# A linear-attention layer and its feed-forward part on one core: a third output buffer, a last batch done row tile by row tile, and a last output sent in halves

## The chip, the cores and the metric

The kernel runs on one core of a Trainium2 chip. The metric is the device time of one execution, in microseconds (us). TensorE (PE) does the matrix products and writes them into PSUM; VectorE (DVE) and ScalarE (ACT) copy, gate and split what PE produced; SyncE (SP) and ACT issue the transfers (DMAs); GpSimd (POOL) only clears memory here.

## The reference

Two steps are computed. The first is a recurrence over 768 positions for 4 batches, 8 heads and a head size of 48, with a state of 48x48 per head. The second is a feed-forward part on the 3072 resulting rows of 384:

```python
for t in range(S):
    cur = einsum('bhd,bhe->bhde', u[None] * k[t], v[t])
    y[t] = einsum('bhd,bhde->bhe', r[t], state + cur)
    state = w * state + einsum('bhd,bhe->bhde', k[t], v[t])
x = y as (4 * 768, 384)
h = x @ w_in                     # 384 -> 2048
g = h * tanh(softplus(h))
out = g @ w_out                  # 2048 -> 384
```

All inputs and the output are float32; the two weights arrive as float64.

## The kernel before

**Tiling.** The 768 positions are cut into 6 groups of 128, and the 4 batches make 4 steps in each group, so a group has 512 columns (`T`). The recurrence is done in chunks of 128 positions by products. For each group, the feed-forward part runs over 16 tiles of 128 hidden rows (`NF`), numbered `n = 16 * g + f` over the whole kernel, 0 to 95. `up_tile(n)` makes one hidden tile `hp` in PSUM; `evacuate` copies it to `hb` (line 890); two tiles make a batch (`FB = 2`, batches 0 to 47), and `gate` applies three activations to a batch (`fa`, lines 785, 788, 791), multiplies (`gate1`, line 798), and, from the second group on, splits the result into a high part `gh` (`gate2`, line 802) and a low part `gl` (`gate3`, line 806). `down_tile(n)` adds the tile's products to three accumulators `acc0`, `acc1`, `acc2` in PSUM, one for each 128 rows of the output (row tile `mt`). In the split form each product is three matmuls (`three`, line 752): high weight by high part, high weight by low part, low weight by high part. `down_tile` comes six tiles (`LAG`) after `up_tile`.

**Outputs.** After the last tile of a group, `output(g, mt)` copies each accumulator to an SBUF tile `ob` (line 825, on ACT or DVE) and sends it with a DMA of 256 KB issued by ACT (line 826). `ob` comes from a pool with two buffers, so the third `ob` of a group takes the buffer of the first, and its copy has to wait until the first one's transfer has landed. Before the first product of the next group, PE needs the accumulators copied out.

**Order.** The order on every engine is written out at build time: `Flow` is a small planner in which each piece of work is a generator that yields the names of events it waits for and a cost in us for one or more engines (`pe(...)`, `act(...)`, `dve(...)`). The planner picks an engine by the time it is free plus the cost, with DVE's cost weighted by 1.5, and emits the instructions in that order; the costs serve this planning alone. At run time each engine goes through its list in order and waits on semaphores.

**Other users.** The tile `we` (two buffers of 128x768) is used in the first group when weights are converted (line 358), and from tile 44 to tile 89 by `check_range`, which reads a weight block every third tile (ACT line 304, DVE line 306). SP issues all loads. ACT and SP, like the other engines, end with a load of a flag (line 986), a branch on it (line 988; the other side is a fallback for unusual inputs, not taken here) and waits for all transfers and engines (lines 988 and 1152).

The recurrence's results are read from PSUM tiles `yt` and `yh` by `finish` (ACT line 700, DVE line 702), and the state update reads another part of `yt` (DVE line 643).

Of the kernel before, what the change touches and what calls it, by code (L numbers as in the profile page):

```python
# [10 lines left out]
F32 = mybir.dt.float32  # L11
# [13 lines left out]
NC = S // C  # L25
NS = NC * B
DM, DFF = H * D, 2048
KT = DM // 128
NF = DFF // 128
# [3 lines left out]
WG = 2  # L33
WE = 384 * WG
NW = NF // WG
# [15 lines left out]
T = B * C  # L51
FB = 2
# [30 lines left out]
LAG = 6  # L83
# [8 lines left out]
L_ATT, L_V, L_IN, L_OUT, L_GATE, L_EVAC, L_PUT, L_FIN = 3, -2, 6, 8, 2, 12, 9, 4  # L92
# [63 lines left out]
def dve(cols, fast=False):  # L156
    return {"dve": 0.14 + cols / (1900 if fast else 950)}


def act(cols):  # L160
    return {"act": 0.1 + cols / 1060}


def pe(us):
    return {"pe": us}
# [3 lines left out]
def rwkv_mish_kernel(ctx, tc, rkT, rkN, vN, wT, w_in, w_out, consts, rkF, vF, wF, uF, outT):  # L169
    nc = tc.nc  # L170
    const = ctx.enter_context(tc.tile_pool(name="const", bufs=1))
    stage = ctx.enter_context(tc.tile_pool(name="stage", bufs=2))
# [107 lines left out]
    flow = Flow(FREE)  # L280
    flow.events["wt"] = 3.5
    at = LAND0
# [48 lines left out]
    raws, whole, parts = {}, {}, {}  # L331
# [407 lines left out]
    def hp_free(cost=None):  # L739

        if cost is None:
            if len(hp_log) >= 2:
                yield hp_log[-2]
            return
        while len(hp_log) >= 2 and hp_log[-2] not in flow.events:
            yield hp_log[-2]
            yield pe(cost)


    def three(out, wh, wl, mh, ml, first, last):  # L750
        for n, (a, m) in enumerate(((wh, mh), (wh, ml), (wl, mh))):
            nc.tensor.matmul(out, lhsT=a, rhs=m, start=first and n == 0, stop=last and n == 2)  # L752
# [4 lines left out]
    def new_batch(T, x, f, n):  # L757

        o = Batch()
        o.T, o.x, o.f, o.n = T, x, f, n  # L760
        o.hb = by_tile(o, work.tile([128, COLS], F32, name="hb", tag="hb", bufs=3))
        return o

    def by_tile(o, t):
        return t[:, : o.n * o.T].rearrange("p (j t) -> p j t", j=o.n)

    def up(o, j, event=None):
        f, T = o.f + j, o.T
        hp = hp_tile("hp", event)
        for k in range(KT):  # L770
            fs = slice((k * WG + f % WG) * 128, (k * WG + f % WG + 1) * 128)
            if o.x.dtype == F32:
                e = whole[0, f // WG]
                nc.tensor.matmul(hp[:, :T], lhsT=e[:, fs], rhs=o.x[:, k, :, 0], start=k == 0, stop=k == KT - 1)  # L774
            else:
                w = parts[0, f // WG]
                three(
                    hp[:, :T], w[:, 0, fs], w[:, 1, fs], o.x[:, k, :, 0], o.x[:, k, :, 1], k == 0, k == KT - 1
                )
        return hp[:, :T]  # L780


    def act1(o):
        o.g = by_tile(o, work.tile([128, COLS], F32, name="fa", tag="fa", bufs=1))
        nc.scalar.activation(o.g, o.hb, AF.Sigmoid, bias=bias_ln2, scale=1.0)  # L785

    def act2(o):
        nc.scalar.activation(o.g, o.g, AF.Arctan)  # L788

    def act3(o):  # L790
        nc.scalar.activation(o.g, o.g, AF.Sin, scale=2.0)  # L791

    def gate1(o):
        if o.x.dtype == F32:
            o.gf = by_tile(o, work.tile([128, COLS], F32, name="gf", tag="gh"))
            nc.vector.tensor_tensor(out=o.gf, in0=o.hb, in1=o.g, op=ALU.mult)  # L796
        else:
            nc.vector.tensor_tensor(out=o.hb, in0=o.hb, in1=o.g, op=ALU.mult)  # L798

    def gate2(o, engine):  # L800
        o.gh = by_tile(o, work.tile([128, COLS], F32R, name="gh", tag="gh"))
        (nc.scalar.copy if engine == "act" else nc.vector.tensor_copy)(out=o.gh, in_=o.hb)  # L802

    def gate3(o):
        o.gl = by_tile(o, work.tile([128, COLS], F32R, name="gl", tag="gl"))
        nc.vector.tensor_tensor(out=o.gl, in0=o.hb, in1=o.gh.bitcast(F32), op=ALU.subtract)  # L806

    accs = {}

    def down(o, j):  # L810
        f = o.f + j
        for mt in range(KT):
# [6 lines left out]
            else:  # L819
                w = parts[1, f // WG]  # L820
                three(a, w[:, 0, ws], w[:, 1, ws], o.gh[:, j], o.gl[:, j], f == 0, f == NF - 1)

    def put(engine, mt, T, cols):
        ob = stage.tile([128, 512], F32, name="ob", tag="ob")
        (nc.scalar.copy if engine == "act" else nc.vector.tensor_copy)(out=ob[:, :T], in_=accs[mt][:, :T])  # L825
        nc.scalar.dma_start(outT[mt * 128 : (mt + 1) * 128, cols], ob[:, :T])


    batches = {}

    def tile_cost(g):
        return pe(9 * (T + 30) / 2400 if g else 3 * 4 * T / 2400)
# [22 lines left out]
    def emitted(n, h):  # L855
        g, f = divmod(n, NF)
        b, j = divmod(n, FB)
        if b not in batches:
            batches[b] = new_batch(T, xs[g], f - j, FB)
        o = batches[b]  # L860
        flow.start(evacuate(n, o, j, h), n - L_EVAC)
        if j == FB - 1:
            flow.start(gate(b, o, range(n - j, n + 1)), n - L_GATE)
        if f == NF - 1:
            flow.set(f"ups{g}")
        if not g and f % WG == WG - 1:
            flow.set(f"used0,{f // WG}")

    def up_tile(n):
        g, f = divmod(n, NF)  # L870
        b, j = divmod(n, FB)
        if n < len(EARLY):
            yield f"early{n}"
            return
        if f == 0:
            for s in range(B):
                yield f"x{g * B + s}"
        if j == 0 and b >= 3:
            yield f"gated{b - 3}"
        yield f"w0,{f // WG}" if g else f"e0,{f // WG}"  # L880
        yield from hp_free()
        yield tile_cost(g)
        yield from hp_free(0.0)
        if j == 0:
            batches[b] = new_batch(T, xs[g], f, FB)
        emitted(n, up(batches[b], j, f"h{n}"))
# [6 lines left out]
    def gate(b, o, tiles):  # L893
        for n in tiles:
            yield f"h{n}"
        if not b:
            yield "TKn"
        if b >= 1:
            yield f"mixed{b - 1}"
        t = act(o.n * o.T)["act"]  # L900
        yield {"act": t + 1.28}
        act1(o)
        yield {"act": t}
        act2(o)
        yield {"act": t + 1.28}
        act3(o)
        if b >= 2:
            yield f"downs{b - 2}"
        cols = o.n * o.T
        yield dve(cols)  # L910
        gate1(o)
        flow.set(f"mixed{b}")
        if b >= NF // FB:
            engine = yield {**act(cols), **dve(cols, True)}
            gate2(o, engine)
            yield dve(cols)
            gate3(o)
        for k in range(o.n):
            flow.set(f"g{FB * b + k}")
        flow.set(f"gated{b}")  # L920

    def down_tile(n):
        g, f = divmod(n, NF)
        b, j = divmod(n, FB)
        if f == 0:
            if g:
                for mt in range(KT):
                    yield f"put{g - 1},{mt}"
            else:
                for k in range(2, len(EARLY)):  # L930
                    yield f"h{k}"
        yield f"w1,{f // WG}" if g else f"e1,{f // WG}"
        yield f"g{n}"
        yield tile_cost(g)
        down(batches[b], j)
        if j == FB - 1:
            flow.set(f"downs{b}")
        if not g and f % WG == WG - 1:
            flow.set(f"used1,{f // WG}")
        if f == NF - 1:  # L940
            for mt in range(KT):
                flow.start(output(g, mt), n - L_PUT)

    def output(g, mt):
        engine = yield {**dve(T), **act(T)}
        put(engine, mt, T, slice(g * T, g * T + T))
        flow.set(f"put{g},{mt}")


    def ffn():  # L950
        last = NC * NF
        for n in range(last + LAG):
            if n < last:
                yield from up_tile(n)
                flow.set(f"u{n}")
            if n >= LAG:
                yield from down_tile(n - LAG)

    load_early()
    for s in range(NS):  # L960
# [13 lines left out]
    for c in range(len(W_ORDER)):  # L974
        i, f = W_ORDER[c]
        flow.start(convert(c), (-999.5, -998.5)[c] if c < 2 else f * WG + (LAG - L_OUT if i else -L_IN) + c / 1000, 0.0)
        flow.start(split(c), NF + f * WG + (LAG - L_OUT if i else -L_IN) + c / 1000, 0.0)
    flow.start(ffn(), 1000, 0.0)
    flow.run()
    assert not flow.parked, list(flow.parked)  # L980
# [7 lines left out]
    with tc.If(in_range < 128 * N_FLAGS):  # L988
# [48 lines left out]
        with tc.tile_pool(name="any2", bufs=1) as work:  # L1037
# [4 lines left out]
            for c, key in enumerate(W_ORDER):  # L1042
                w = parts[key]
# [6 lines left out]
                    out=eu, in0=top, scalar=0x80000000, in1=eu, op0=ALU.bitwise_and, op1=ALU.bitwise_xor  # L1050
# [8 lines left out]
            for b in range(B):  # L1059
                with tc.For_i(0, S, 128) as t0:  # L1060
# [5 lines left out]
                    for k in range(KT):  # L1066
                        nc.tensor.transpose(
                            out=t[:, k * 128 : (k + 1) * 128], in_=xt[:, k].rearrange("t q e -> t (q e)"), identity=unit32
# [4 lines left out]
                    for f in range(0, NF, 4):  # L1073
                        o = new_batch(128, x, f, 4)
# [82 lines left out]
```

## Time and profile before

| | us |
|---|---|
| median of 3 runs | 511.91 (511.68 to 512.68) |
| time of the profiled execution | 512.17 |
| span of the profiled execution | 510.3 |
| PE busy | 495.0 (97%) |
| ACT busy | 412.9 (81%) |
| DVE busy | 372.4 (73%) |
| granted TensorE clock, mean | 0.987 |

The span is the time from the first to the last instruction in the trace; the time of an execution is 1.9 us longer. Busy time counts instructions of the engine, not those of its sequencer (loads of registers, branches, waits, issues of DMAs). In a timeline, `ACT L825 COPY ob<-acc [2.61 <-DMA out_dram<-ob]` means that ACT, at line 825, copied `acc` to `ob` after 2.61 us of idling that a DMA out of `ob` ended; a `q` behind an engine's name marks its sequencer.

### The profile page before, as it was taken

Reading aid. Unit: us, or ns where it says so; the run is one execution under the profiler, and the core shown is the slowest. Engines: PE = TensorE matmul, PEld = TensorE weight load, DVE = VectorE, ACT = ScalarE, POOL = GpSimd, SP = SyncE. Lnnn points to the kernel's source line nnn. Section 1 sums busy time; section 2 is a strip of 40 time slices with the busy share of each in tenths; the row PEclk is TensorE's granted clock in tenths of the full one; section 3 lists DMA queues with packets and bytes.
Section 4 is the critical chain, followed back from the end, with each engine's and each line's share of the span. In section 5 each row is a group of like instructions: output and inputs, shape, how many; then the busy total and the mean of one; then the engine's idle time right before and its main releaser. Section 6 shows DMA issues by size and latency. Waiting matters only on the chain. (4 is left out here: it accounts for less than half of the span.)

```text
span 510.3 us, 9022 instructions
## 1 busy us (share of the span) xinstructions
PE 495.0 (97%) x3651; PEld 382.8 (75%) x3651; DVE 372.4 (73%) x592; ACT 412.9 (81%) x521; POOL 2.1 (0%) x9
## 2 busy tenths in 40 slices
PE   7999999999999999999999989999999999999993
PEld 5796555556678888888888868888888888888872
DVE  6898898898878986778785868885877545645431
ACT  3759996668888988897878778979888889989880
POOL 1000000000000000000000000000000000000000
PEclk8799999999999999999999999999999999999998
DMA  8999423220253020245034443424442213111001
GB/s 260 379 374 396 129 79 98 88 69 5 83 151 104 1 83 22 89 132 162 23 84 144 151 128 125 124 77 151 150 148 82 73 65 122 66 62 63 2 1 67
DMA packets 19442, 58.86 MB, mean 115 GB/s; under 512 B 3072, under 2 KB 3584, under 8 KB 19392
## 3 DMA queue, kind: packets, MB, share of 16 engines
q1 hardware_dynamic: 16656, 53.10, 32.2%
q10 hardware_dynamic: 2736, 5.10, 2.8%
q8 instruction: 31, 0.51, 0.4%
q14 instruction: 19, 0.16, 0.1%
HBM read 51.50 MB, written 4.72 MB: 110 GB/s over the span
## 5 line engine op out<-in xcount | busy, mean ns | idle before, releaser
L752 PE MATMUL hp<-x,w 128*128 128x512 f32 x720 | 181.0, 396 | 2.4 <-DVE hb L890 2.2
L752 PE MATMUL acc<-gh,w 128*128 128x512 f32 x480 | 160.2, 390 | 0.5 <-DVE gh L802 0.5
L752 PEld LDWEIGHTS hp<-x,w 128*128 128x128 f32 x720 | 133.8, 188 | 34.0 <-issue 2.8
L752 PEld LDWEIGHTS acc<-gh,w 128*128 128x128 f32 x480 | 90.1, 188 | 19.6 <-DVE gh L802 0.9
L752 PE MATMUL acc<-gl,w 128*128 128x512 f32 x240 | 93.6, 390 | 0.8 <-DVE gl L806 0.8
L798 DVE TENSOR_TENSOR hb<-hb,fa 128x1024 f32<-128x1024 f32 x40 | 48.9, 1223 | 56.2 <-ACT fa L791 56.1
L785 ACT ACT_TABLE_LOAD x48 | 61.6, 1283 | 8.3 <-DVE gf L796 7.5
L791 ACT ACT_TABLE_LOAD x48 | 61.6, 1283 | 0.8
L890 ACT COPY hb<-hp 128x512 f32<-128x512 f32 x66 | 38.5, 584 | 24.9 <-PE hp L752 19.7
L785 ACT ACTIVATE fa<-hb,small 128x1024 f32<-128x1024 f32 x48 | 55.4, 1153 | 0.6
L752 PEld LDWEIGHTS acc<-gl,w 128*128 128x128 f32 x240 | 45.1, 188 | 10.9 <-DVE gl L806 1.5
L806 DVE TENSOR_TENSOR gl<-hb,gh 128x1024 fp32r<-128x1024 f32 x40 | 48.9, 1222 | 4.1 <-ACT gh L802 3.6
L788 ACT ACTIVATE fa<-fa 128x1024 f32<-128x1024 f32 x48 | 50.9, 1060 | 1.0
L791 ACT ACTIVATE fa<-fa 128x1024 f32<-128x1024 f32 x48 | 50.9, 1061 | 0.5
L818 PE MATMUL acc<-gf,wraw 128*128 128x512 f32 x96 | 43.8, 592 | 0.0
L553 DVE COPY_PREDICATED P<-cst,pa 128x512 f32<-128x512 uint32 x48 | 34.8, 731 | 3.7 <-PE pa L534 3.2
L890 DVE COPY hb<-hp 128x512 f32<-128x512 f32 x30 | 20.7, 690 | 22.6 <-PE hp L752 17.4
L802 ACT CAST gh<-hb 128x1024 fp32r<-128x1024 f32 x20 | 21.1, 1054 | 16.4 <-DVE hb L798 15.0
L818 PEld LDWEIGHTS acc<-gf,wraw 128*128 128x128 f32 x96 | 18.8, 196 | 20.0 <-issue 19.1
L774 PE MATMUL hp<-x,wraw 128*128 128x512 f32 x72 | 33.1, 600 | 0.0
L460 DVE TENSOR_TENSOR rk<-rk,TRK 112x512 f32<-112x512 f32 x44 | 29.9, 683 | 0.7 <-DMA rk<-in_rkT_dram 0.7
L774 PEld LDWEIGHTS hp<-x,wraw 128*128 128x128 f32 x72 | 13.7, 196 | 14.7 <-issue 14.2
(101 smaller groups left out, 524.2 us busy)
## 6 DMA issues: line engine op xcount, KB each, us to landing
wraw<-in_w_in_dram SPq DMA_DIRECT2D x16, 768.0 KB, 6.3
wraw<-in_w_out_dram SPq DMA_DIRECT2D x16, 768.0 KB, 7.8
rk<-in_rkT_dram SPq DMA_DIRECT2D x22, 448.0 KB, 4.2
rkn<-in_rkN_dram SPq DMA_DIRECT2D x20, 384.0 KB, 4.3
v<-in_vN_dram SPq DMA_DIRECT2D x22, 256.0 KB, 4.1
out_dram<-ob ACTq DMA_DIRECT2D x18, 256.0 KB, 2.4
x<-st SPq DMA_DIRECT2D x60, 32.0 KB, 1.9
rkx<-in_rkT_dram SPq DMA_DIRECT2D x2, 448.0 KB, 10.9
```

What stands on the lines that cost most here:

```text
L460: nc.vector.tensor_tensor(out=rk[:112, a], in0=rk[:112, a], in1=TRK[:112, a], op=ALU.mult)
L553: nc.vector.copy_predicated(out=Ps[s][:, :, i].rearrange("j (w z) i -> j w z i", w=2), mask=masks.unsqueeze(2).broadcast_to([128, 2, NP // ...
L752: nc.tensor.matmul(out, lhsT=a, rhs=m, start=first and n == 0, stop=last and n == 2)
L774: nc.tensor.matmul(hp[:, :T], lhsT=e[:, fs], rhs=o.x[:, k, :, 0], start=k == 0, stop=k == KT - 1)
L785: nc.scalar.activation(o.g, o.hb, AF.Sigmoid, bias=bias_ln2, scale=1.0)
L788: nc.scalar.activation(o.g, o.g, AF.Arctan)
L791: nc.scalar.activation(o.g, o.g, AF.Sin, scale=2.0)
L798: nc.vector.tensor_tensor(out=o.hb, in0=o.hb, in1=o.g, op=ALU.mult)
L802: (nc.scalar.copy if engine == "act" else nc.vector.tensor_copy)(out=o.gh, in_=o.hb)
L806: nc.vector.tensor_tensor(out=o.gl, in0=o.hb, in1=o.gh.bitcast(F32), op=ALU.subtract)
L818: nc.tensor.matmul(a, lhsT=whole[1, f // WG][:, ws], rhs=o.gf[:, j], start=f == 0, stop=f == NF - 1)
L890: (nc.scalar.copy if engine == "act" else nc.vector.tensor_copy)(out=o.hb[:, j], in_=h)
```

## The change

There are three parts.

1. A new helper `out_buffer(mt)` gives the outputs of row tiles 0 and 1 an `ob` as before and that of row tile 2 a `we` tile.
2. The last batch of the kernel (47, tiles 94 and 95) is not done by two calls of `down_tile` but by `down_last`: after an event `high47`, set between `gate2` and `gate3`, it does the four matmuls with `gh` for row tile 0, then the four for row tile 1; after `gated47` it does the two with `gl` for row tile 0, the two for row tile 1, and then all six for row tile 2. Each row tile's output is started as soon as its last product is emitted. `ffn`'s loop is rewritten so that all other tiles come in the order they had.
3. The very last output (group 5, row tile 2) goes through `put_halves`: 256 columns are copied by ACT and sent by a DMA that ACT issues, 256 columns are copied by DVE and sent by a DMA that SP issues.

```diff
+    def out_buffer(mt):
+        if mt < 2:
+            return stage.tile([128, 512], F32, name="ob", tag="ob")
+        return stage.tile([128, WE], F32, name="we", tag="we", bufs=2)
+
     def put(engine, mt, T, cols):
-        ob = stage.tile([128, 512], F32, name="ob", tag="ob")
+        ob = out_buffer(mt)
...
+    def put_halves(mt, at):
+        ob, n = out_buffer(mt), T // 2
+        for k, (copy, queue) in enumerate(((nc.scalar.copy, nc.scalar), (nc.vector.tensor_copy, nc.sync))):
+            h = slice(k * n, (k + 1) * n)
+            yield (act if not k else dve)(n)
+            copy(out=ob[:, h], in_=accs[mt][:, h])
+            queue.dma_start(outT[mt * 128 : (mt + 1) * 128, at + k * n : at + (k + 1) * n], ob[:, h])
...
             gate2(o, engine)
+            flow.set(f"high{b}")
             yield dve(cols)
             gate3(o)
...
+    def down_last(b):
+        o, w = batches[b], parts[1, NW - 1]
+        n = FB * b + o.n - 1
+        def products(mt, low):
+            for j in range(o.n):
+                f = o.f + j
+                ws = slice(f % WG * DM + mt * 128, f % WG * DM + (mt + 1) * 128)
+                for k in range(1 if low else 2):
+                    nc.tensor.matmul(
+                        accs[mt][:, :T], lhsT=w[:, k, ws], rhs=(o.gl if low else o.gh)[:, j], start=False,
+                        stop=low and f == NF - 1,
+                    )
+        yield "w1,%d" % (NW - 1)
+        yield f"high{b}"
+        yield pe(1.85)
+        for mt in range(2):
+            products(mt, False)
+        yield f"gated{b}"
+        for mt in range(KT):
+            yield pe(0.46 if mt < 2 else 1.4)
+            if mt == 2:
+                products(mt, False)
+            products(mt, True)
+            flow.start(output(NC - 1, mt), n - L_PUT)
+
     def output(g, mt):
+        if (g, mt) == (NC - 1, KT - 1):
+            yield from put_halves(mt, g * T)
+            return
...
     def ffn():
-        last = NC * NF
-        for n in range(last + LAG):
-            if n < last:
-                yield from up_tile(n)
-                flow.set(f"u{n}")
-            if n >= LAG:
-                yield from down_tile(n - LAG)
+        last, done = NC * NF, 0
+        for n in range(last):
+            yield from up_tile(n)
+            flow.set(f"u{n}")
+            while done <= n - LAG:
+                yield from down_tile(done)
+                done += 1
+        while done < last - FB:
+            yield from down_tile(done)
+            done += 1
+        yield from down_last(last // FB - 1)
```

## The prediction

> **What bounds the kernel now.** I read the page first for the span, then the windows for PE's share by stretch, then the waits, and then the timeline at each place where PE waited.
>
> ```profile
> span 510.3 us, 9022 instructions
> ```
>
> ```profile
> 306.00:490.00 184.00, 184.00 (x1130) 151.53 (x1130) 115.69 (x182) 161.91 (x190) 0.00 (x0) 1.00 0.28 91
> ```
>
> The second row is a window of 184.00 us: its width, then PE, PE's weight loads, DVE, ACT and POOL busy, the granted clock (1.00), the DMA share and GB/s. PE is busy in all of it. Between 306 and 490 us nothing but a shorter list of matmuls could gain anything, and what PE gains ahead of 306 is carried to the end if the others follow. So the change can act at PE's few waits and at the end. The waits of the whole run (total, times, longest) name them:
>
> ```profile
> ACT ob L825 <- DMA out_dram<-ob: 5.5, 4, 2.6
> ...
> ACT x L700 <- DVE S L643: 2.5, 4, 1.3
> ...
> PE hp L752 <- DVE hb L890: 2.2, 1, 2.2
> ...
> DVE ob L825 <- DMA out_dram<-ob: 2.2, 1, 2.2
> ```
>
> Five group boundaries have a third output copy that sat on ACT or DVE until the first output had landed. One PE wait of 2.2 us stands beside them, and the timeline shows that it belongs to the longest of the five:
>
> ```profile
> 299.02 0.34 ACTq L826 DMA_DIRECT2D out_dram<-ob  x1
> ...
> 301.60 0.59 ACT L825 COPY ob<-acc 128x512 f32<-128x512 f32 x1 [2.61 <-DMA out_dram<-ob]
> ...
> 302.60 0.27 ACT L700 CAST st<-yh 128x128 fp32r<-128x128 f32 x1 [0.41 <-ACT ob L825]
> ...
> 302.90 0.29 DVE L702 TENSOR_TENSOR st<-yh,st 128x128 fp32r<-128x128 f32 x1 [3.20 <-ACT st L700]
> ...
> 303.84 1.23 DVE L806 TENSOR_TENSOR gl<-hb,gh 128x1024 fp32r<-128x1024 f32 x1 [0.41 <-ACT gh L802]
> 304.99 0.68 DVE L890 COPY hb<-hp 128x512 f32<-128x512 f32 x1
> ```
>
> ```profile
> 302.92 0.39 PE L752 MATMUL acc<-gl,w 128*128 128x512 f32 x1
> 303.15 0.39 PE L752 MATMUL acc<-gh,w 128*128 128x512 f32 x1
> 305.73 2.33 PE L752 MATMUL hp<-x,w 128*128 128x512 f32 x9 [2.19 <-DVE hb L890]
> 307.90 0.39 PE L752 MATMUL acc<-gh,w 128*128 128x512 f32 x1
> ```
>
> The copy held ACT; behind it on ACT stood the cast of `st`; DVE waited 3.20 us for that; behind it on DVE stood the copy of a hidden tile; and PE waited 2.19 us for that copy's PSUM buffer. At the first boundary the same happens in small:
>
> ```profile
> 143.36 0.34 ACTq L826 DMA_DIRECT2D out_dram<-ob  x1
> 144.49 0.59 ACT L825 COPY ob<-acc 128x512 f32<-128x512 f32 x1 [1.17 <-DMA out_dram<-ob]
> ```
>
> ```profile
> 149.53 0.73 PE L752 MATMUL hp<-x,w 128*128 128x512 f32 x2 [0.21 <-ACT hb L890]
> ```
>
> At the end, the timeline:
>
> ```profile
> 497.86 1.23 DVE L806 TENSOR_TENSOR gl<-hb,gh 128x1024 fp32r<-128x1024 f32 x1
> ...
> 497.88 0.49 PE L752 MATMUL acc<-gh,w 128*128 128x512 f32 x1 [0.52 <-DVE gh L802]
> ...
> 499.14 0.50 PE L752 MATMUL acc<-gl,w 128*128 128x512 f32 x1 [0.77 <-DVE gl L806]
> ...
> 501.31 0.39 PE L752 MATMUL acc<-gl,w 128*128 128x512 f32 x1
> ...
> 501.96 0.59 ACT L825 COPY ob<-acc 128x512 f32<-128x512 f32 x1 [6.19 <-PE acc L752]
> ...
> 502.58 1.12 ACTq L826 DMA_DIRECT2D out_dram<-ob  x2
> 502.64 0.69 DVE L825 COPY ob<-acc 128x512 f32<-128x512 f32 x1 [3.56 <-PE acc L752]
> ...
> 502.90 0.39 PE L752 MATMUL acc<-gh,w 128*128 128x512 f32 x1
> 505.06 0.59 ACT L825 COPY ob<-acc 128x512 f32<-128x512 f32 x1 [2.51 <-SPq L988]
> 505.68 0.34 ACTq L826 DMA_DIRECT2D out_dram<-ob  x1
> ```
>
> PE idles twice before the last batch (0.52 and 0.77), is done at 502.90 + 0.39 = 503.29, and the third copy starts only at 505.06. The releaser named, SP's line 988, is SP's own wait for the same transfer: the first output, issued at 502.58. After the last issue the sequencers still have work, which the lines 986, 988 and 1152 show:
>
> ```profile
> L988 ACTq COMPARE_BRANCH  x1: 54/54/54, 506.6 to 506.6; - x1
> L988 ACTq EVENT_SEMAPHORE  x1: 17/17/17, 509.4 to 509.4; - x1
> ```
>
> ```profile
> L988 SPq EVENT_SEMAPHORE  x3: 17/17/17, 505.0 to 508.2; - x3
> ```
>
> ```profile
> L986 SPq TENSOR_LOAD <-small x1: 476/476/476, 475.6 to 475.6; - x1
> ```
>
> ```profile
> L988 SPq EVENT_SEMAPHORE  x5: 17/17/17, 479.1 to 479.4; - x5
> ```
>
> ```profile
> L1152 SPq EVENT_SEMAPHORE  x8: 28/28/807, 508.2 to 508.7; - x8
> ```
>
> ACT's branch at 506.6 is followed by nothing until 509.4: 2.8 us to get to the instruction behind it. SP's last landing was seen at 508.2, its eight line-1152 waits reach 508.7, and the last of them takes 0.81, until ACT arrives. So ACT's issue at 505.68 sets the end: 3.7 us to 509.4, then 0.9 to 510.3. SP did its own flag load and branch at 475.6, long before, in time that cost nothing.
>
> **The change part by part.**
>
> Third buffer, third boundary. The copy can start when ACT's issue at 299.02 is over, 299.36, plus the 0.04 that ACT takes after an issue (302.22 + 0.34 to 302.60): 299.40 for 301.60, so ACT is 2.20 early. DVE waited for ACT, so its copy at 304.99 goes to 302.79 and ends at 303.47; PE's matmul before the wait ends at 303.15 + 0.39 = 303.54. The 2.19 goes, just. The nine matmuls after the wait took 307.90 - 305.73 = 2.17, against 9 x 0.227 = 2.04 at PE's running pace (302.92 to 303.15): 0.13 more. Gain 2.3. If the gain stops short, DVE's copy is late next, by hundredths.
>
> Third buffer, first boundary: the copy moves from 144.49 to 143.74, which covers PE's 0.21. Taken 0.2, ends 0 and 0.35 (with a slower start like the 0.13). The other three boundaries have no PE wait behind them: nothing. After 306 all others wait for PE or run behind it, so I let the whole order move with it. Sum of the middle 2.5, ends 0 and 2.7. The `we` tile brings a wait for an older check or an older output, both many tiles old: nothing.
>
> Last batch. PE starts at 497.88 as before, since `gh` is ready then. Eight matmuls without `gl` take 8 x 0.23 = 1.8, to 499.7, and `gl` is ready at 497.86 + 1.23 = 499.09, so the second idle goes. From 499.14 to the last start at 502.90 before were 16 steps, 3.76; eighteen matmuls now have 17, 3.76 + 0.23 = 3.99: the last ends at 497.88 + 3.99 + 0.39 = 502.26 (503.29 before). `acc0` has its tenth matmul by 497.88 + (501.31 - 499.14) + 0.39 = 500.44, `acc1` its twelfth by 500.89.
>
> Copies. ACT copies `acc0` 500.48 to 501.07 (0.59) and issues to 501.44. By the planner's costs the second goes to ACT too (0.58 + 0.58 = 1.17 against 0.46 + 1.5 x 0.68 = 1.48): 501.48 to 502.07, issued to 502.44. Were it DVE, all that follows would be about 0.15 earlier. The halves' nearest rows are reads of 128x256 from PSUM:
>
> ```profile
> L700 ACT CAST x<-yt x20: 350/373/393, 66.0 to 414.8; 128x256 fp32r<-128x256 f32 x20
> L702 DVE TENSOR_TENSOR x<-yt,x x20: 408/418/427, 66.8 to 416.3; 128x256 fp32r<-128x256 f32 x20
> ```
>
> Taken 0.37 and 0.42; the ends are half of a whole copy and all of it (0.30 to 0.59, 0.35 to 0.69). ACT's half runs 502.48 to 502.85, issued at 502.88. Do both run at once? In the waits, ACT's cast of `x` (line 700) waited four times, 2.5 us, for DVE's state update (line 643). The two write different tiles and only share the PSUM tile `yt` that they read. So two engines' reads of one accumulator are put in order, and DVE's half comes second: 502.88 to 503.30, SP's issue at 503.33.
>
> The Trainium skill, "PSUM — Partial Sum Buffer", section "PSUM bank collisions raise a hardware error", says the same in general: two engines must not read one bank at once, also in disjoint columns, and software has to order them. With that rule and the row agreeing, the halves cannot overlap; without it the sum would be that of the second rival.
>
> The end. ACT: 502.88 + 3.7 = 506.6 at its last wait. SP: the issue (0.34, as ACT's) and 0.04 to 503.71; from the flag load to the first wait behind the branch 479.1 - 475.6 = 3.5, to 507.2; eight line-988 waits at 0.08 (four steps in 479.1 to 479.4), to 507.8; the eight line-1152 waits 0.5, to 508.3; and the 0.8 from 509.5 to 510.3 that closes the kernel: 509.1. The landing of SP's half (2.4, the median below) is in by 505.8 and hidden. So SP, moved from nothing to last, sets the end at 509.1 for 510.3: gain 1.2. Ends: 0.5 (the longest copies, and a jump of 2.8 as on ACT) and 1.8 (halves at once).
>
> The Trainium skill, "Advanced Engine Details and Errata", section "Control Flow Timing", gives about 108 ns for compare-and-branch. By that figure SP would end some 2.5 us sooner, an estimate; the rows show 2.6 on SP (476.5 to 479.1) and 2.8 on ACT, so the measurement decides and I give it no chance.
>
> Sum: 2.5 + 1.2 = 3.7. The profiled execution took 512.17, so 508.5; the median, 511.91, is 0.26 below it, so 508.2.
>
> **Rivals.**
>
> The halves run side by side: DVE's half 502.30 to 502.72, SP's issue 502.75, end 508.5, and 507.6 in all. For it: both are only reads. Against it: the 2.5 us of line 700.
>
> Another wait takes the place of PE's 2.19: the gap between DVE's copy (303.47) and PE's need (303.54) is 0.07, and behind it ACT has 161.91 of 184 busy. If everything gained there is lost again, the tail's 1.2 stays: 510.7. Against it: from 306 on the others idle for PE, so they follow it.
>
> Slower: the output's `we` tile makes a check wait for an output's landing. The place is the fourth boundary:
>
> ```profile
> 378.38 0.91 ACT L304 ACTIVATE we<-wraw 128x768 f32<-128x768 f32 x1 [1.43 <-DVE ob L825]
> ```
>
> ```profile
> DMA to landing us min/median/max: 2.0/2.4/6.3
> ```
>
> The third output there would be issued near 377.4 and land 2.0 to 6.3 later; a check that took its buffer would hold ACT from about 377.7 to between 379.4 and 383.7. At the third boundary a hold of 2.20 cost PE 2.19, so it would cost 1.7 to 6.0 us; from 4.7 on the kernel is slower by more than a measurement tells, and at 6.0 it takes 514.2. Against it: two buffers are taken in turn, and that check gets the one of the check before, not the output's.
>
> **How the numbers follow.** The forecast, 508.2, has 0.55, with its own range 507.3 to 509.3; halves at once 0.10; the stall replaced 0.20; the check 0.04; the other 0.11 is a part of the 2.3 lost again, 509 to 510.8. The range 507.2 to 510.8 leaves out the check, part of the lowest and part of the highest cases. A change of 0.2%, 1.0 us, is about what a measurement of this kernel can tell from none. Faster than 510.9: 0.55 + 0.10 + 0.12 of the stall's 0.20 + 0.08 = 0.85; within 1.0 us 0.10; slower 0.05.
>
> **What would show it.** The middle: no third copy waiting for `out_dram<-ob`, no PE wait near 303.5, and everything behind it 2.5 us earlier. The last batch: one PE idle before it, `gl` no longer a releaser, PE done about 4.4 after its start. The halves: DVE's after ACT's. The end: SP's flag load behind its issue, nothing for 2.6 us after its branch, and SP's line-1152 waits the last to start. The prediction is wrong if PE waits elsewhere between 303 and 490, if the halves overlap, or if ACT and not SP ends last.

## The result and the profile after

The changed kernel takes 507.67 us (median; 507.34 to 508.34), against 512.08 for the kernel before in the same comparison: the ratio is 0.9915, 95% interval 0.9898 to 0.9932. Timed again beside the kernels of experiments 6 and 7 it came to 508.48 against 512.18, 0.9918 (0.9891 to 0.9945). The forecast was 508.2, 3.7 us less; measured are 4.4 and 3.7 us less.

Page and windows of the profile after:

```profile
span 505.8 us, 9021 instructions
```

```profile
302.40:486.00 183.60, 183.60 (x1128) 151.24 (x1128) 115.90 (x181) 161.60 (x189) 0.00 (x0) 1.00 0.28 91
```

From the third boundary on PE is as full as before: 183.60 us busy of 183.60. The two spans differ by 4.5 us, but 0.6 of that is no effect of the change. It arises in the first 19 us, where the two traces had another granted clock: the same matmul starts at 18.58 before and at 17.97 after. The window from 5 to 17.1 us shows the clock (third figure from the end), 0.64 before in the first row, 0.74 after in the second:

```profile
5.00:17.10 12.10, 9.55 (x110) 7.19 (x110) 11.76 (x27) 7.48 (x23) 0.00 (x0) 0.64 1.03 322
```

```profile
5.00:17.10 12.10, 8.55 (x108) 6.34 (x107) 11.70 (x28) 7.76 (x23) 0.00 (x0) 0.74 1.03 338
```

Without these 0.6 the traces differ by 3.9: 2.7 in the middle and 1.2 at the end.

**The middle.** PE's waits of the whole run after, all of them:

```profile
PE sd L479 <- DVE q L471: 2.6, 1, 2.6
PE hp L864 <- DVE wraw L362: 1.0, 1, 1.0
PE pa L534 <- DVE rk L460: 0.9, 1, 0.9
PE pa L268 <- DVE small L196: 0.9, 1, 0.9
PE acc L970 <- DVE gh L802: 0.5, 1, 0.5
```

The 2.2 us on `hb` and the 0.2 at the first boundary are gone, and so is `gl`. The timeline at the third boundary, ACT, then DVE, then PE:

```profile
297.88 0.34 ACTq L832 DMA_DIRECT2D out_dram<-ob  x1
298.26 0.59 ACT L831 COPY we<-acc 128x512 f32<-128x512 f32 x1 [0.41 <-PE yt L654]
298.88 0.34 ACTq L832 DMA_DIRECT2D out_dram<-we  x1
299.26 0.27 ACT L700 CAST st<-yh 128x128 fp32r<-128x128 f32 x1 [0.41 <-ACT we L831]
```

```profile
299.56 0.29 DVE L702 TENSOR_TENSOR st<-yh,st 128x128 fp32r<-128x128 f32 x1 [1.00 <-ACT st L700]
...
301.65 0.69 DVE L905 COPY hb<-hp 128x512 f32<-128x512 f32 x1
```

```profile
302.02 0.39 PE L752 MATMUL acc<-gh,w 128*128 128x512 f32 x1
302.39 0.96 PE L752 MATMUL hp<-x,w 128*128 128x512 f32 x3
```

The third copy, now into `we`, starts 0.04 us after the issue before it. DVE's wait for `st` is 1.00 instead of 3.20. PE still pauses a little: 302.02 to 302.39 is 0.37 between two starts, where PE's pace is 0.23. No wait is printed, since a matmul's modelled end (0.39 behind its start) covers it. Before, the same two starts were 303.15 and 305.73, 2.58 apart; so 2.2 us are gained.

**The end.** Timeline after, PE, ACT, DVE, SP:

```profile
494.55 2.11 PE L970 MATMUL acc<-gh,w 128*128 128x512 f32 x8 [0.52 <-DVE gh L802]
496.50 1.08 PE L970 MATMUL acc<-gl,w 128*128 128x512 f32 x4
...
498.32 0.61 PE L970 MATMUL acc<-gl,w 128*128 128x512 f32 x2
```

```profile
497.16 0.59 ACT L831 COPY ob<-acc 128x512 f32<-128x512 f32 x1 [4.72 <-PE acc L970]
...
498.21 0.59 ACT L831 COPY ob<-acc 128x512 f32<-128x512 f32 x1 [0.47 <-ACT ob L831]
...
499.21 0.37 ACT L840 COPY we<-acc 128x256 f32<-128x256 f32 x1 [0.41 <-PE acc L970]
```

```profile
499.61 0.43 DVE L840 COPY we<-acc 128x256 f32<-128x256 f32 x1 [3.86 <-ACT we L840]
```

```profile
500.07 0.34 SPq L841 DMA_DIRECT2D out_dram<-we  x1
```

PE runs through the last batch without its second wait; DVE's half sits until ACT's half is done. The sequencers behind that, with the flag load now at line 1037, the branch at 1039 and the closing waits at 1203:

```profile
L1037 SPq TENSOR_LOAD <-small x1: 480/480/480, 472.2 to 472.2; - x1
```

```profile
L1039 SPq EVENT_SEMAPHORE  x8: 17/17/17, 503.9 to 504.4; - x8
L1039 SPq COMPARE_BRANCH  x1: 45/45/45, 500.5 to 500.5; - x1
...
L1039 ACTq EVENT_SEMAPHORE  x1: 17/17/17, 504.0 to 504.0; - x1
```

```profile
L1203 SPq EVENT_SEMAPHORE  x8: 28/28/28, 504.5 to 504.9; - x8
```

SP loaded its flag at 472.2, ahead of its issue, but it branches at 500.5, behind it, reaches the next instruction 3.4 us later, and then goes through eight waits and eight more. All take next to no time, but one after the other they fill 503.9 to 505.0; nothing waits for ACT any more. SP ends last. The transfer that SP issued at 500.07 took 3.3 us to land; its first wait behind the branch, which is for this transfer, comes at 503.9, after the landing.

### The profile page after: what moved, and what is told of

Its sections match the earlier page's. It is cut to its first block, busy times and chain, and to the rows that moved or that the text cites. A ratio compares the mean times of both kernels' runs of the same rounds, so it can differ in the third digit from the quotient of the medians.

```text
span 505.8 us, 9021 instructions
## 1 busy us (share of the span) xinstructions
PE 492.9 (97%) x3651; PEld 381.4 (75%) x3651; DVE 372.3 (74%) x592; ACT 413.3 (82%) x522; POOL 2.1 (0%) x9
## 4 chain that ended last, share of the span: by engine, by line
PE 93%; ACT 3%; DVE 2%; issue 1%; DMA 1%; ACTq 0%; DVEq 0%
PE hp L752 33%; PE acc L752 29%; PE acc L818 8%; PE hp L774 6%; PE pa L534 3%; PE yh L594 2%; PE hp L864 2%; PE yt L585 2%; PE yt L594 2%; PE yt L654 1%; PE yt L568 1%; DMA small<-in_wT_dram 1%; PE yt L570 1%; PE idle L268 1%; PE acc L970 1%
## 5 line engine op out<-in xcount | busy, mean ns | idle before, releaser
L752 PE MATMUL acc<-gh,w 128*128 128x512 f32 x468 | 156.2, 389 | 0.0
L752 PEld LDWEIGHTS acc<-gh,w 128*128 128x128 f32 x468 | 87.8, 188 | 18.3
L752 PE MATMUL acc<-gl,w 128*128 128x512 f32 x234 | 91.1, 389 | 0.0
L752 PEld LDWEIGHTS acc<-gl,w 128*128 128x128 f32 x234 | 43.9, 188 | 9.6 <-DVE gl L806 0.4
```

## The experiments

To compare the ends of kernels whose middles differ, the distance from the first product with the last batch's `gh` to the last instruction is used and called the tail; its start is the PE row with the wait for `gh` (497.88 before, 494.55 after). Before it is 12.4 us, after 11.2.

| kernel | median us | before, same chip | ratio, 95% interval | tail in its trace |
|---|---|---|---|---|
| the change | 507.67 | 512.08 | 0.9915 (0.9898 to 0.9932) | 11.25 |
| 1 buffer alone | 508.46 | 511.66 | 0.9926 (0.9899 to 0.9953) | 10.99 |
| 2 last batch alone | 510.84 | 511.66 | 0.9983 (0.9962 to 1.0004) | 10.94 |
| 3 halves alone | 513.04 | 511.66 | 1.0024 (1.0004 to 1.0045) | 12.80 |
| 4 all but the halves | 507.52 | 511.66 | 0.9899 (0.9868 to 0.9930) | 10.68 |
| 5 the change again | 508.48 | 512.18 | 0.9918 (0.9891 to 0.9945) | 11.21 |
| 6 as 4, second copy on DVE | 507.94 | 512.18 | 0.9914 (0.9888 to 0.9940) | 10.69 |
| 7 both halves issued by ACT | 507.92 | 512.18 | 0.9908 (0.9883 to 0.9934) | 11.20 |
| 8 DVE's half from `acc0` | one run | | | 9.93 |
| 9 as 4, no branch | one run | | | 8.11 |
| 10 the change, no branch | one run | | | 8.15 |
| 11 as 4, second trace | one run | | | 10.70 |

**1. The third buffer alone.** The kernel before with this edit:

```diff
+    def out_buffer(mt):
+        if mt < 2:
+            return stage.tile([128, 512], F32, name="ob", tag="ob")
+        return stage.tile([128, WE], F32, name="we", tag="we", bufs=2)
...
-        ob = stage.tile([128, 512], F32, name="ob", tag="ob")
+        ob = out_buffer(mt)
```

> Only the third buffer (the output of row tile 2 takes a we tile), the last batch and the last output as before. Theory: the buffer brings all of the middle (0.5 us at the first boundary, 2.2 at the third), and at the end the third copy starts near 503.4 instead of 505.06 in the time of before, another 1.7: 4.4 us less than before, about 507.6. Rival: the gain seen ahead of the last batch is mostly the clock of the first 17 us, which differed between the two traces, and the buffer brings only the 1.7 at the end: about 510.3.

The buffer alone has the ratio 0.9926: 3.8 us of 512 by it (4.4 expected), most of the change. PE's waits in its trace, all of them:

```profile
PE sd L479 <- DVE q L471: 2.2, 1, 2.2
PE hp L855 <- DVE wraw L362: 1.0, 1, 1.0
PE pa L534 <- DVE rk L460: 0.9, 1, 0.9
PE pa L268 <- DVE small L196: 0.9, 1, 0.9
PE acc L752 <- DVE gl L806: 0.8, 1, 0.8
PE acc L752 <- DVE gh L802: 0.5, 1, 0.5
```

Neither the wait on `hb` nor that of the first boundary is there; the one for `gl` still is. The tail is 1.4 us shorter (1.7 expected). So the middle comes from the buffer; the rival falls. At the end, too, the buffer alone has a shorter tail (11.0) than all three parts together (11.2).

**2. The last batch alone.** `down_last`, the event `high47` and the new loop, with every output in `ob` and whole.

> Only the new order of the last batch; all outputs use ob's two buffers and the last output is whole. Theory: the first copy starts 1.5 us earlier, its transfer lands 1.5 earlier, and since the third copy still waits for that landing, the end moves by the same 1.5: about 510.5. Rival: what counts is the end of the products, 1.0 us earlier: about 511.0. In both the middle is as before, with PE's wait of 2.2 us.

PE's 2.2 us in the middle is there again, as it should be, and the tail is 1.5 us shorter. The third copy still waits for the first landing (timeline of ACT):

```profile
500.52 0.59 ACT L829 COPY ob<-acc 128x512 f32<-128x512 f32 x1 [4.72 <-PE acc L968]
...
503.85 0.59 ACT L829 COPY ob<-acc 128x512 f32<-128x512 f32 x1 [1.70 <-SPq L1034]
```

The first copy starts 2.6 us into the tail instead of 4.1, and the third 5.95 instead of 7.2. The time, 0.9 us less with an interval that reaches 1.0004, is smaller than the trace's 1.5 and does not decide between the two readings; the trace speaks for the landing.

**3. The halves alone.** `put_halves` with an `ob` tile, in the kernel before:

```diff
     def output(g, mt):
+        if (g, mt) == (NC - 1, KT - 1):
+            yield from put_halves(mt, g * T)
+            return
```

> Only the last output in halves, from an ob tile that waits for the first transfer as before. Theory: the half that SP issues puts SP's branch behind it and DVE's half runs after ACT's, so the end comes 1.0 to 1.3 us later than before: about 513.2. Rival: half copies and half transfers are shorter and hide the branch: 0.3 us less than before, about 511.8.

By the ratio it is slower by 0.0004 to 0.0045, on the theory's side. The tail is only 0.4 us longer, not 1.0 to 1.3, and the rest of that trace was slower by other things (granted clock 0.981). So the halves do not help; how much they cost is not settled by this run.

**4. All but the halves.** The changed kernel without the three lines in `output` that call `put_halves`.

> Third buffer and new order of the last batch, the last output whole, copied and sent by ACT or DVE as the planner puts it. Theory: without the half that SP issues the branch of SP is early again; ACT's issue near 499.8 in the time of after is followed by 3.7 us to ACT's last wait and 0.85 to the end, 504.4 against 505.8: 1.3 us faster than with the halves, about 506.4. Rival: the halves shorten the end: 0.3 us slower than with them, about 508.0.

The tail is 0.6 us shorter than with the halves, not 1.3, and the time's interval overlaps the change's. ACT's last wait came where the theory had it, 8.9 us into the tail, but the last landing, which SP waits for, was later still, at 9.3:

```profile
L1036 ACTq EVENT_SEMAPHORE  x1: 17/17/17, 504.4 to 504.4; - x1
L1036 SPq EVENT_SEMAPHORE  x1: 17/17/17, 504.8 to 504.8; - x1
```

That is 4.0 us after the issue, where 2.0 had been the least. It asked for a cause.

**5. The change again**, as a partner for the next two.

> The changed kernel itself, timed beside the next two. Theory and rival alike: about 4.4 us less than before. From the first product with the last batch's gh to the end the trace of after had 11.25 us, with SP's branch last; here 10.6 to 11.3, by how long SP's jump and the landings take.

As expected: ratio and tail repeat.

**6. The second copy on DVE.** In the kernel of experiment 4:

```diff
-        engine = yield {**dve(T), **act(T)}
+        engine = yield dve(T) if (g, mt) == (NC - 1, 1) else {**dve(T), **act(T)}
```

> Third buffer and new order of the last batch, the last output whole, and the second output of the last group copied by DVE. Theory: ACT is free when the third accumulator is done, so its copy starts 4.42 us after the first product of the last batch (4.66 with the second copy on ACT) and its issue comes at 5.04 (5.27); landing plus 1.4 us sets the end, 8.5 to 10.4 us after that product, by the landing: 0.2 us faster than the same kernel with the second copy on ACT, and 0.6 to 1.0 faster than the change as made. Rival: the copies do not count, since the landing of the transfers varies by more: no difference from the change as made.

The third issue did come 0.24 us earlier, 5.03 into the tail, and the landing was at 9.31, where it had been. Nothing is gained by an earlier issue. By time there is no difference from the change, as the rival said; the tail is 0.5 us shorter than the change's, as in experiment 4.

**7. Both halves issued by ACT.** In the change:

```diff
-... (nc.vector.tensor_copy, nc.sync))
+... (nc.vector.tensor_copy, nc.scalar))
```

> The change as made, but both halves of the last output are issued by ACT; SP has nothing to issue at the end. Theory: SP's branch, late, is what the halves cost. Here it is early again and the end is ACT's: second issue 5.52 us after the first product of the last batch, ACT's last wait near 9.1, end 9.9 to 10.3 us after that product (11.25 in the trace of after), about 1.0 us faster than the change as made. Rival: the cost of the halves is the order of the copies and the landings, which stay: 11.0 to 11.3, no faster.

My theory fell here. SP's branch is early again, and the tail is 11.20 all the same. What came last is the fourth transfer:

```profile
DMA to landing us min/median/max: 1.7/2.8/3.8
```

```profile
L1039 SPq EVENT_SEMAPHORE  x8: 17/17/17, 504.5 to 505.0; - x8
```

ACT's first half landed 1.7 us after its issue, the second 3.8. And SP's list of waits starts with the fourth transfer's semaphore: SP stood at the head of the list until 504.5, and the whole list, sixteen waits in 1.0 us, came behind the landing. With three transfers (the kernel before, experiments 1, 2, 4 and 6) the last landing is the eighth wait of the list, and seven of them are over by then. In experiments 4 and 6 that landing is at 9.3 as well, so the seven waits more behind it here (at 0.06 to 0.1 us each) are the 0.5 us by which their tails are shorter.

**8. DVE's half from another accumulator.** In the change:

```diff
-            copy(out=ob[:, h], in_=accs[mt][:, h])
+            copy(out=ob[:, h], in_=accs[0 if k else mt][:, h])
```

> The change as made, but DVE's half of the last output is copied from acc0 instead of acc2, so that half of the last row tile's output is left out (it holds columns of row tile 0). Theory: DVE's half came after ACT's because both read one accumulator in PSUM. Reading acc0 it waits only for ACT's copy of acc0 and starts about 3.25 us after the first product of the last batch, ahead of ACT's half (5.07 in the trace of after, right behind it). Rival: the two halves are put in order by the we tile that both write: DVE's half still starts right behind ACT's, at about 5.07.

```profile
497.41 0.59 ACT L831 COPY ob<-acc 128x512 f32<-128x512 f32 x1 [4.73 <-PE acc L970]
```

```profile
498.03 0.43 DVE L840 COPY we<-acc 128x256 f32<-128x256 f32 x1 [2.03 <-ACT ob L831]
```

DVE's half now waits for ACT's copy of `acc0` alone (497.41 + 0.59 = 498.00) and writes its half of `we` 1.4 us before ACT writes the other. So it is the accumulator that both read, not the tile that both write, that puts the halves in order. The tail is 9.93, with SP's issue 1.8 us earlier than in the change, but half of the last row tile's output is left out, so this is no kernel to use.

**9 and 10. No branch.** Flag load, branch and fallback are left out, in the kernel of experiment 4 and in the change.

> Third buffer and new order of the last batch, last output whole; the flag load, the branch and the fallback behind it are left out. Theory: the 16 KB fetch of code that PE's branch sets off holds one DMA engine for 0.9 to 1.7 us near 6.3 us after the first product of the last batch, and one sixteenth of the last transfer waits behind it; so does the kernel. Without a branch there is no fetch: the last transfer, issued at 5.27, lands 2.0 to 2.4 later, 7.3 to 7.7, and the end comes 1.4 behind, 8.7 to 9.1 (10.68 with the branch). Rival: the last transfer lands late because it follows two others of 256 KB: landing stays at 8.6 to 9.3 and the end at 10.0 or later.

> The change as made, but the flag load, the branch and the fallback behind it are left out. Theory: what the halves cost against the whole (0.5 us in the traces) is that a fourth transfer's landing comes first in SP's list of waits, so the list of sixteen, 1.0 us, runs after it; the landing itself is no later. Here SP issues at 5.51, it lands by 7.9, and the end comes 1.4 to 1.9 behind: 9.0 to 9.8. Rival: the halves cost by SP's branch alone; without a branch they are as fast as the whole or faster, at most 9.0.

Both tails shrink by about 2.6 and 3.1 us and are the same: 8.11 and 8.15. The last transfer of experiment 9, issued 5.27 us into the tail, lands 2.0 later:

```profile
out_dram<-we ACTq DMA_DIRECT2D x1, 256.0 KB, 2.0
```

It still follows two others of 256 KB, so those are not what made it late. In experiment 10 the theory's 9.0 to 9.8 missed, and the rival's figure, at most 9.0, came true; experiment 7 speaks against the rival's reason, SP's branch alone. Without the branch SP has few waits left, so the order of its list costs nothing, and the halves, issued 5.54 us in, land at the same 7.28 as the whole. Halving gains nothing even there: DVE's half comes second, and its issue, at 5.54, is later than that of the whole, at 5.27.

**11. The kernel of experiment 4 again.**

> A second trace of the kernel with the third buffer, the new order of the last batch and the whole last output. Theory: the last transfer's final sixteenth waits again behind the fetch near 6.3 us after the first product of the last batch; landing 8.6 to 9.4, end 10.0 to 10.8. Rival: the late landing of the first trace (4.0 us after its issue) was chance: landing by 7.9, end set by ACT's jump at 9.8.

The landing took 4.1 us again. The DMA queues of this run point to the cause, first in the 1.8 us from 501.35 to 503.14, then from 503.1 to 504.2 (packets, MB, share of 16 engines; q10 carries ACT's transfers; the packets of q8 and q14 are instructions, that is, code):

```profile
q10 hardware_dynamic: 139, 0.25, 38.1%
q8 instruction: 1, 0.02, 6.2%
q14 instruction: 1, 0.01, 1.6%
```

```profile
q10 hardware_dynamic: 9, 0.02, 5.9%
```

A single packet of code on q8 fills one of the 16 engines for the whole window: 6.2% of 16 x 1.79 is 1.8 us (the one on q14 takes 0.5). Fifteen sixteenths of the output go on beside it; nine packets, one sixteenth of the output's 144, come after it. The trace does not name the engine, so that these nine stood behind this packet is inferred; experiment 9, where the packet is missing and the landing takes 2.0, agrees. The page's q8 line has 31 packets for 0.51 MB, 16 KB each; that of experiment 9 has 29, and none of them is in the tail. With the branch the landing comes 9.3 us into the tail in experiments 4, 6, 7 and 11, with issues from 5.03 to 5.52, so in these four an earlier issue did not move it. The packet starts about 6 to 7 us into the tail of every kernel with the branch; that PE fetches it, whose branch is the only one early enough in all of them, is likely but was not tried alone.

## Why the prediction was right

The mechanism held in the middle. At the end the sum is right partly by luck.

- **Third buffer, third boundary: right.** 2.3 forecast, 2.2 measured. The 0.13 for the slow restart was a mistake: a pause of 0.37 is left, and PE starts slowly after it all the same.
- **First boundary: too small.** 0.2 forecast with an upper end of 0.35; start to start it gave 0.48. The step that failed took 0.21 from the wait as printed. The starts were 148.93 and 149.53, 0.60 apart, and are now 0.22; the rest is the slower restart. Middle in all: 2.7 measured, 2.5 forecast.
- **The other boundaries and the `we` tile: right.** No PE wait appeared, no check waits for an output, and everything behind 303 moved with PE.
- **Last batch: right.** From first to last start 4.00 us (forecast 3.99, before 5.02), `gl` no longer a releaser.
- **Copies: right, in order and in time.** Into the tail: first copy 2.61 (forecast 2.60), second 3.66 (3.60), ACT's half 4.66 (4.60), DVE's half 5.06 (5.00), SP's issue 5.52 (5.45). That the halves run one after the other, and that it is for the accumulator they share, experiment 8 shows. It agrees with what the prediction quotes from the Trainium skill, "PSUM — Partial Sum Buffer", section "PSUM bank collisions raise a hardware error": that software has to keep two engines from reading one bank at once. No run here shows such reads at once, so what would come of them stays open. The "second rival" that the prediction names there is the first in its list.
- **The end: the right sum from two wrong terms.** SP ends last, 11.25 us into the tail (forecast 11.2). But its flag load does not stand behind its issue: it ran at 472.2, so that 0.9 us was not paid. And its jump took 3.4 us, not 2.6. That the two nearly cancel is luck. The landing of SP's half took 3.3, not 2.4, and stayed hidden behind the jump. The step that failed is the one that carried SP's rows of before, taken when PE was deep in its products, to the end of the kernel.
- **What the halves cost** is some 0.5 us by the traces (11.2 against 10.7, two traces each), and not through SP's late branch alone: with that gone, in experiment 7, the fourth transfer's late landing and its place at the head of SP's list cost as much. By time the two cannot be told apart.
- **The parts of the end were not priced one by one.** The buffer alone takes 1.4 us off the tail, the last batch alone 1.5, both together 1.7, and the halves give 0.5 of that back, so the 1.2 of the end is less than the buffer brings there alone.
- **No version beat the change measurably.** The kernel of experiment 4 has the shorter tail and less code, and that of experiment 1 has only the buffer; both have ratios whose intervals overlap the change's.

## What to carry to other kernels

When two buffers serve three outputs, look past the copy that waits to what is queued behind it: here 2.6 us of ACT's waiting became 3.2 on DVE and 2.2 on PE, and one more buffer took nearly all of it. For PE count from start to start, since printed waits leave out what a modelled end covers. At the end of a kernel the last copy is not the end: follow the landing, the branch and the list of closing waits, and add no transfer there that a shorter path does not need. Run each part of a change alone: here one of three brought most of the gain.

## What the runs showed of the hardware that I had not expected

- A packet of code on q8 has 16 KB and takes one of 16 DMA engines 0.9 (experiment 6) to 1.8 us (experiment 11). A 256 KB output under way at that time landed 4.0 to 4.3 us after its issue (experiments 4, 6, 11), against 2.0 without such a packet (experiment 9).
- From a taken branch to the next instruction SP, ACT and DVE took between 2.4 (ACT, experiment 1) and 3.6 us (DVE, the change). It was 2.6 on SP in mid-kernel before, and 3.3 to 3.4 in both traces of the change, where three engines branched within 0.1 us. In experiment 3, where they branched within 0.3, it was 2.8 to 3.1; whether they slow each other stays open.
- SP's closing waits cost 0.06 to 0.1 us each even when all is long done, so sixteen are 1.0 us, and the place of the last transfer's semaphore in their order decides how many come after it.
